# A gated recurrence and a perceptron on one core: weights rounded with an integer add, and the transposes around the scan split into single steps

## The chip, the core and the metric

The kernel runs on one core of one Trainium2 chip. The engines are TensorE (PE in the rows; PEld is its loading of weights), VectorE (DVE), ScalarE (ACT), GpSimd (POOL, which here issues the weights' DMAs) and SyncE (SP, which issues the other DMAs). The metric is the device time of one execution in microseconds. The time before is the median of three runs, 892.08 us (891.6 to 896.12).

## The reference

```python
def _attn_ref(q, k, v, a_re, a_im):              # (4, 8, 768, 48)
    mag = np.sqrt(a_re * a_re + a_im * a_im)
    scale = np.minimum(mag, 0.999) / (mag + 1e-06)
    a_re_n, a_im_n = (a_re * scale, a_im * scale)
    for t in range(S):
        new_re = ar * S_re - ai * S_im
        new_im = ar * S_im + ai * S_re
        kv = np.einsum('bhd,bhe->bhde', k[:, :, t], v[:, :, t])
        S_re, S_im = (new_re + kv, new_im)
        y[:, :, t] = np.einsum('bhd,bhde->bhe', q[:, :, t], S_re)

def _moe_ref(x, w_in, w_out):                    # x = y as (3072, 384)
    h = x @ w_in                                 # w_in (384, 2048)
    r = np.maximum(h, 0.0)
    g = r * r
    return (g @ w_out).astype(np.float32)        # w_out (2048, 384)
```

The two weights reach the kernel in 64-bit floats; all else is 32-bit.

## The kernel before

The sequence is cut into 8 units: 4 batches, 2 halves of 384 positions each. The recurrence of a unit is turned into running products of the gates and ordinary masked products of scores. Each unit passes through three lists of work.

- **The chain** (`chain_work`) is mostly VectorE and ScalarE: `load`; `normalise` for each half z of the heads; `measure`, three ScalarE sums of squares into a throw-away tile `junk`; `inner` and `inverse` for each z, which end with the tile `last` (L691, L692); `totals`, in which TensorE transposes the three parts j of `last` (4 transposes each, tile `tot`, L721), ScalarE copies the first two into `e` (L723) and VectorE makes running products of the third into `x` (L726); `scan`, some 70 small VectorE operations on `e` (L754, L757, L758); `back`, in which TensorE transposes e and x back (12 transposes, tile `bk`, L790) and ScalarE copies them to `xn` (L791); and `apply` for each z (L801 to L813), whose output `QK` is what the next list reads.
- **The pair list** (`pair_work`) takes four pairs of heads i: `turn` transposes QK (tile `tq`, L825, copied by L828), `keep` makes the state for the second half (`kv`), `score` makes masked scores (`sa`, `sb`; VectorE L843, L851 and ScalarE copies), `mix` multiplies them with v (`ypair`, L878 and L882), and the result goes by DMA into `xT`.
- **The dense list** (`dense_work`) has 16 items `hidden` (tile `h`, 3 products each, L913, with two ScalarE passes L916 and L917) and 12 items `project` (tile `o`, 4 products each, L925).

`merge` interleaves lists evenly: item i of a list with n items stands at (i + 0.5)/n. The program is: chain of unit 0 alone; pair list of unit 0 merged with `convert` of pieces 0 to 15; chain of unit 1 merged with `convert` of pieces 16 to 31; then, for each unit n, its dense list merged with the pair list of unit n+1 and the chain of unit n+2. Every engine runs its own instructions in one fixed order, which a list scheduler derives from this program and may move up where buffers allow. The PSUM pool `trp` with two buffers (tag `tr`) serves `tot`, `bk`, `tq` and `kv` together.

`convert(i)` brings one of 32 pieces of the weights (128 x 384 numbers of 64 bits) into the buffer `raw` by a GpSimd DMA and makes 32-bit floats of it with five VectorE operations (L576, L578, L580, L582, L584): two put sign, exponent and mantissa of the upper word in place, two scale the lower word to the last place, one adds the two.

Of the kernel before, what the change touches and what calls it, by code (L numbers as in the profile page):

```python
# [9 lines left out]
F32 = mybir.dt.float32  # L10
I32 = mybir.dt.int32
U32 = mybir.dt.uint32
BF16 = mybir.dt.bfloat16
AF = mybir.ActivationFunctionType
ALU = mybir.AluOpType
PSUM = bass.MemoryType.PSUM
# [463 lines left out]
def fast_path(ctx, tc, q, k, v, a_re, a_im, moe_w_in, moe_w_out, out, flag):  # L480
# [10 lines left out]
    nc = tc.nc  # L491
    B, H, S, D = q.shape
    C = 128
# [18 lines left out]
    pr = ctx.enter_context(tc.tile_pool(name="pr", bufs=2))  # L512
    gp = ctx.enter_context(tc.tile_pool(name="gp", bufs=NF))
    xp = ctx.enter_context(tc.tile_pool(name="xp", bufs=2))
    wst = ctx.enter_context(tc.tile_pool(name="wst", bufs=2))
    trp = ctx.enter_context(tc.tile_pool(name="trp", bufs=2, space=PSUM))
    scp = ctx.enter_context(tc.tile_pool(name="scp", bufs=2, space=PSUM))
    yp = ctx.enter_context(tc.tile_pool(name="yp", bufs=1, space=PSUM))
# [44 lines left out]
    def convert(i):  # L563

        dst, src = piece(i)
        if not wide:
            nc.gpsimd.dma_start(
                out=dst.rearrange("p (m f) -> p m f", m=src.shape[1]), in_=src)
            return
        raw = wst.tile([C, DM, 2], U32, name="raw", tag="raw")  # L570
        nc.gpsimd.dma_start(
            out=raw.rearrange("p (m f) two -> p m (f two)", m=src.shape[1]), in_=src)
        lo, hi = raw[:, :, 0], raw[:, :, 1]
        bits = dst.bitcast(U32)
        more = wst.tile([C, DM], U32, name="more", tag="more")
        dve.tensor_scalar(out=bits, in0=hi, scalar1=0x07FFFFFF, scalar2=3,  # L576
                          op0=ALU.bitwise_and, op1=ALU.logical_shift_left)
        dve.scalar_tensor_tensor(out=bits, in0=hi, scalar=0xC0000000, in1=bits,  # L578
                                 op0=ALU.bitwise_and, op1=ALU.bitwise_or)
        dve.tensor_scalar(out=more, in0=bits, scalar1=0xFF800000, scalar2=None,  # L580
                          op0=ALU.bitwise_and)
        dve.scalar_tensor_tensor(out=more.bitcast(F32), in0=lo, scalar=2.0 ** -52,  # L582
                                 in1=more.bitcast(F32), op0=ALU.mult, op1=ALU.mult)
        dve.tensor_tensor(out=dst, in0=dst, in1=more.bitcast(F32), op=ALU.add)  # L584

    SPARE = ("fa0", "fa1", "fb0", "fb1")

# [106 lines left out]
    def measure(u):  # L694

        for j, t in enumerate((whole(u["qk", 0]), whole(u["qk", 1]),
                               u["v"].rearrange("p j h d -> p (j h d)"))):
            junk = wst.tile([C, H * W * D], BF16, name="junk", tag="junk", bufs=1)
            act.activation(out=junk, in_=t, func=AF.Square,
                           accum_out=sums[:, u["n"], 4 + j:5 + j])  # L700

    carry = {}

    def totals(u):


        e = u["e"] = wk.tile([R, 2, NP, C + 1], F32, name="e", tag="e")
        x = u["x"] = wk.tile([R, NP, C + 1], F32, name="x", tag="x")
        if u["half"] == 0:
            dve.memset(e[:, 0, :, 0], SCALE)  # L710
            dve.memset(e[:, 1, :, 0], 0.0)
            dve.memset(x[:, :, 0], SCALE ** -2)
        else:
            dve.tensor_copy(out=e[:, :, :, 0], in_=carry["e"])
            dve.tensor_copy(out=x[:, :, 0], in_=carry["x"])
        last = u["last"]
        for j in range(3):
            src = last[:, j].rearrange("p (i h) d -> p i (h d)", i=NP)
            ps = trp.tile([R, NP, C], F32, name="tot", tag="tr")
            for i in range(NP):  # L720
                nc.tensor.transpose(ps[:, i], src[:, i], ident)  # L721
            if j < 2:
                act.copy(out=e[:, j, :, 1:C + 1], in_=ps)  # L723
            else:
                for i in range(NP):
                    dve.tensor_tensor_scan(out=x[:, i, 1:C + 1], data0=ps[:, i],  # L726
                                           data1=ones, initial=x[:, i, 0:1],
                                           op0=ALU.mult, op1=ALU.bypass)
        n = u["n"]
        dve.scalar_tensor_tensor(out=grow[0:R, n], in0=x[:, :, 0], scalar=2.0 ** 124,  # L730
                                 in1=x[:, :, C], op0=ALU.mult, op1=ALU.is_ge)
        if u["half"] == NHALF - 1:
            dve.tensor_scalar(out=total[0:R, u["b"]], in0=x[:, :, C], scalar1=2.0 ** 124,
                              scalar2=None, op0=ALU.is_le)
        else:
            carry["x"] = wk.tile([R, NP], F32, name="cx", tag="cx")
            dve.tensor_copy(out=carry["x"], in_=x[:, :, C])
# [22 lines left out]
    def scan(u):  # L760

        e = u["e"]
        body = e[:, :, :, 0:C]
        v8 = body.rearrange("p r i (g w) -> p r i g w", w=8)
        for w in range(1, 8):
            product(u, v8[:, :, :, :, w], v8[:, :, :, :, w - 1], v8[:, :, :, :, w])
        v32 = v8[:, :, :, :, 7].rearrange("p r i (g w) -> p r i g w", w=4)

        inc = wk.tile([R, 2, NP, 16], F32, name="inc", tag="inc")
        i4 = inc.rearrange("p r i (g w) -> p r i g w", w=4)  # L770
        dve.tensor_copy(out=inc, in_=v8[:, :, :, :, 7])
        for w in range(1, 4):
            product(u, i4[:, :, :, :, w], i4[:, :, :, :, w - 1], i4[:, :, :, :, w])
        for g in range(1, 4):
            prev = i4[:, :, :, g - 1, 3]
            for_all = prev.unsqueeze(3).to_broadcast([R, 2, NP, 4])
            product(u, i4[:, :, :, g], i4[:, :, :, g], for_all)
        for i in range(NP):
            y = inc[:, :, i, 0:15].unsqueeze(3).to_broadcast([R, 2, 15, 8])
            product(u, v8[:, :, i, 1:16], v8[:, :, i, 1:16], y)  # L780
        if u["half"] < NHALF - 1:
            carry["e"] = wk.tile([R, 2, NP], F32, name="ce", tag="ce")
            product(u, carry["e"], e[:, :, :, C - 1], e[:, :, :, C])

    def back(u):
        xn = u["xn"] = wk.tile([C, 3, H, D], F32, name="xn", tag="xn")
        for j, src in enumerate((u["e"][:, 0], u["e"][:, 1], u["x"])):
            ps = trp.tile([C, NP, R], F32, name="bk", tag="tr")
            for i in range(NP):
                nc.tensor.transpose(ps[:, i], src[:, i, 0:C], ident[0:R, 0:R])  # L790
            act.copy(out=xn[:, j].rearrange("p (i h) d -> p i (h d)", i=NP), in_=ps)  # L791

    def apply(u, z):

# [142 lines left out]
    def chain_work(u):  # L937
        return ([lambda: load(u)] + [lambda z=z: normalise(u, z) for z in range(2)]
                + [lambda: measure(u)]
                + [lambda z=z, f=f: f(u, z) for f in (inner, inverse) for z in range(2)]  # L940
                + [lambda: totals(u), lambda: scan(u), lambda: back(u)]
                + [lambda z=z: apply(u, z) for z in range(2)])


# [103 lines left out]
```

## Time and profile before

| | us |
|---|---|
| median of 3 runs | 892.08 |
| profiled execution | 891.34 |
| its span, first to last instruction | 889.6 |
| TensorE busy | 769.7 |
| VectorE busy | 550.4 |
| ScalarE busy | 421.4 |
| GpSimd busy | 43.7 |

The profiled execution is one run on its own, so its 891.34 differs a little from the median. Of it, 889.6 us are the span and 1.7 lie around it. Busy times overlap, since the engines run side by side. The mean granted clock of TensorE is .977 of full speed.

### The profile page before, as it was taken

The page shows a single profiled execution, that of the slowest core. Times are in us where ns is not written, and L with a number is a line of the kernel's source. Part 1 is how long each engine was busy: PE and PEld are TensorE (multiplying, and loading weights), DVE is VectorE, ACT ScalarE, POOL GpSimd, SP SyncE. Part 2 cuts the span into 40 slices and gives each one's busy share as a digit, 9 for nine tenths or more (in the row PEclk, how much of TensorE's full clock was granted, in tenths as well). Part 3 has the DMA queues.
Part 4 walks back from the last instruction along what each step waited for, and adds up shares of the span by engine and source line. Part 5 has one row for each costly group of instructions (what it writes and reads, how often), then busy time and mean ns, then how long its engine had stood idle before and what let it go on. Part 6 is the DMA issues. An engine that isn't in the chain of part 4 may idle for free.

```text
span 889.6 us, 9241 instructions
## 1 busy us (share of the span) xinstructions
PE 769.7 (87%) x3138; PEld 462.7 (52%) x3138; DVE 550.4 (62%) x1415; ACT 421.4 (47%) x833; POOL 43.7 (5%) x76
## 2 busy tenths in 40 slices
PE   0106989987898989998999899998999889999996
PEld 0004645443455655664666555564666545555553
DVE  4998899988987697338760877168652876400000
ACT  5303845067378329731784239621973215411510
POOL 1020111000000000000000000000000034100000
PEclk9999999998998999999999999998999999999999
DMA  9134443240130033000500132002300068400000
GB/s 239 36 98 128 141 139 108 71 116 13 41 107 7 17 96 96 7 16 16 148 8 8 36 115 50 7 16 62 104 7 7 15 181 270 149 16 31 1 9 22
DMA packets 76920, 61.24 MB, mean 69 GB/s; under 512 B 28736, under 2 KB 71744, under 8 KB 76864
## 3 DMA queue, kind: packets, MB, share of 16 engines
q1 hardware_dynamic: 70720, 35.40, 14.4%
q0 software_dynamic: 6144, 25.17, 9.3%
q8 instruction: 26, 0.43, 0.2%
q14 instruction: 30, 0.25, 0.1%
HBM read 51.12 MB, written 4.72 MB: 63 GB/s over the span
## 4 chain that ended last, share of the span: by engine, by line
PE 49%; DVE 23%; issue 13%; DMA 9%; ACT 4%; POOL 1%; SPq 0%; POOLq 0%; ACTq 0%
PE h L913 19%; PE o L925 14%; DVE fa L754 7%; PE ypair L882 4%; PE sa L839 4%; DVE QK L813 2%; PE tq L825 2%; DMA raw<-in_moe_w_in_dram 2%; DVE e L757 2%; PE ypair L878 2%; DMA look<-in_moe_w_in_dram 2%; DMA raw<-in_moe_w_out_dram 2%; PE sb L849 2%; DMA look<-in_moe_w_out_dram 1%; PE sa L841 1%
## 5 line engine op out<-in xcount | busy, mean ns | idle before, releaser
L913 PE MATMUL h<-xT,w 128*128 128x384 f32 x768 | 272.1, 494 | 9.0 <-DMA xT<-yt 5.1
L925 PE MATMUL o<-w,g 128*128 128x384 f32 x768 | 263.7, 489 | 1.6 <-DVE w L584 1.5
L925 PEld LDWEIGHTS o<-w,g 128*128 128x128 f32 x768 | 140.7, 190 | 87.6 <-DVE w L584 4.1
L913 PEld LDWEIGHTS h<-xT,w 128*128 128x128 f32 x768 | 139.1, 192 | 89.6 <-issue 10.5
L843 DVE TENSOR_TENSOR A<-sa,mask 128x256 f32<-128x256 f32 x64 | 26.8, 422 | 131.5 <-PE sa L841 131.3
L828 ACT COPY QKT<-tq 96x512 f32<-96x512 f32 x96 | 80.9, 854 | 41.3 <-PE tq L825 41.2
L916 ACT ACTIVATE g<-h 128x384 f32<-128x384 f32 x128 | 62.4, 491 | 73.7 <-PE h L913 73.7
L825 PE MATMUL tq<-ident,QK 128*96 128x128 f32 x384 | 61.2, 286 | 10.7 <-DVE QK L813 7.2
L917 ACT ACTIVATE g<-g 128x384 f32<-128x384 f32 x128 | 66.7, 525 | 2.3
L825 PEld LDWEIGHTS tq<-ident,QK 128*96 128x96 f32 x384 | 45.4, 132 | 39.5 <-issue 21.1
L882 PE MATMUL ypair<-A,v 128*48 128x256 f32 (+2 forms) x384 | 63.1, 410 | 0.0
L839 PE MATMUL sa<-QKT 96*128 96x384 f32 x128 | 55.8, 518 | 3.7 <-ACT QKT L828 3.7
L844 ACT COPY A<-sa 128x256 f32<-128x256 f32 x64 | 23.6, 372 | 59.3 <-DVE A L843 59.0
L929 ACT COPY ot<-o 128x384 f32<-128x384 f32 x24 | 11.5, 478 | 84.3 <-PE o L925 84.2
L721 PE MATMUL tot<-ident,last 128*96 128x128 f32 x96 | 15.8, 293 | 39.5 <-ACT last L691 35.0
L790 PE MATMUL bk<-ident,e 96*128 96x96 f32 x64 | 14.7, 311 | 40.0 <-DVE e L757 39.8
L791 ACT COPY xn<-bk 128x384 f32<-128x384 f32 x24 | 10.9, 480 | 73.5 <-PE bk L790 73.5
L754 DVE TENSOR_TENSOR fa<-e 96x128 f32<-96x128 f32 (+1 forms) x120 | 39.9, 366 | 8.2 <-ACT e L723 6.9
L813 DVE TENSOR_TENSOR QK<-qk,a 128x576 f32<-128x576 f32 x64 | 44.1, 750 | 0.0
L882 PEld LDWEIGHTS ypair<-A,v 128*48 128x48 f32 x384 | 27.1, 130 | 31.5 <-issue 23.2
L991 DVE TENSOR_SCALAR flag<-cnt 1x1 int32<-1x1 f32 x1 | 0.1, 147 | 69.1 <-PE cnt L990 69.1
L596 POOL DMA_DIRECT2D look<-in_moe_w_in_dram x16 | 12.2, 761 | 566.2 <-DVE a L807 555.4
(106 smaller groups left out, 975.8 us busy)
## 6 DMA issues: line engine op xcount, KB each, us to landing
raw<-in_moe_w_in_dram POOLq DMA_DIRECT2D x16, 384.0 KB, 3.7
raw<-in_moe_w_out_dram POOLq DMA_DIRECT2D x16, 384.0 KB, 3.3
look<-in_moe_w_in_dram POOLq DMA_DIRECT2D x16, 384.0 KB, 4.3
look<-in_moe_w_out_dram POOLq DMA_DIRECT2D x16, 384.0 KB, 4.1
a<-in_a_re_dram SPq DMA_DIRECT2D x16, 288.0 KB, 3.0
a<-in_a_im_dram SPq DMA_DIRECT2D x16, 288.0 KB, 3.4
qk<-in_q_dram SPq DMA_DIRECT2D x16, 288.0 KB, 4.3
qk<-in_k_dram SPq DMA_DIRECT2D x16, 288.0 KB, 4.5
```

The source lines that it names most:

```text
L754: dve.tensor_tensor(out=t, in0=x, in1=y[:, j].unsqueeze(1).to_broadcast(shape), op=ALU.mult)
L813: dve.tensor_tensor(out=t[:, j, :, :, r], in0=qk[:, j], in1=a[:, r], op=ALU.mult)
L825: nc.tensor.transpose(ps[:, 2 * j + h], src[:, j, (2 * i + h) % HH, c].rearrange("p r d -> p (r d)"), ident)
L828: act.copy(out=u["T"][i].rearrange("r z (p c) -> r c z p", c=W)[:, c], in_=ps)
L839: nc.tensor.matmul(sa[:, 0:3].rearrange("p n t -> p (n t)"), lhsT=kt[:, 0:C], rhs=qt, start=True, stop=True)
L843: dve.tensor_tensor(out=A[:, h, 0:4:3], in0=sa[:, 0:4:3], in1=mask2, op=ALU.mult)
L844: act.copy(out=A[:, h, 1:3], in_=sa[:, 1:3])
L882: nc.tensor.matmul(ypair[64 * h:64 * h + D, j * C:L], lhsT=u["v"][:, j, 2 * i + h], rhs=A[:, h, lo:hi].rearrange("p n t -> p (n t)"), star ...
L913: nc.tensor.matmul(ps, lhsT=w1[:, f, m], rhs=u["xT"][:, m], start=(m == 0), stop=(m == NM - 1))
L916: act.activation(out=t, in_=ps, func=AF.Relu)
L917: act.activation(out=t, in_=t, func=AF.Square)
L925: nc.tensor.matmul(u["o"], lhsT=u["g"][f][:, ts(c, C)], rhs=w2[:, f], start=(f == 0), stop=(f == NF - 1))
```

## The change

`convert` keeps the two operations that build the upper part. The lower word is no longer masked, multiplied and added as a float. ScalarE multiplies it by 2^-29 and writes it as an integer, which rounds it to the last place of the 32-bit mantissa, and VectorE adds this as an integer to the bits of the upper part. The pool `wst` has three buffers `raw` instead of two. The tile `more` keeps two buffers and now shares them with `junk`, which becomes an 8-bit float so that it fits. `totals` and `back` do one part j per call, so that the chain list has 17 items instead of 13, and the groups of four transposes stand apart in the merged program.

```diff
-    wst = ctx.enter_context(tc.tile_pool(name="wst", bufs=2))
+    wst = ctx.enter_context(tc.tile_pool(name="wst", bufs=3))
...
-        more = wst.tile([C, DM], U32, name="more", tag="more")
+        more = wst.tile([C, DM], U32, name="more", tag="more", bufs=2)
+        act.activation(out=more, in_=lo, func=AF.Copy, scale=2.0 ** -29)
         dve.tensor_scalar(out=bits, in0=hi, scalar1=0x07FFFFFF, scalar2=3,
                           op0=ALU.bitwise_and, op1=ALU.logical_shift_left)
         dve.scalar_tensor_tensor(out=bits, in0=hi, scalar=0xC0000000, in1=bits,
                                  op0=ALU.bitwise_and, op1=ALU.bitwise_or)
-        dve.tensor_scalar(out=more, in0=bits, scalar1=0xFF800000, scalar2=None,
-                          op0=ALU.bitwise_and)
-        dve.scalar_tensor_tensor(out=more.bitcast(F32), in0=lo, scalar=2.0 ** -52,
-                                 in1=more.bitcast(F32), op0=ALU.mult, op1=ALU.mult)
-        dve.tensor_tensor(out=dst, in0=dst, in1=more.bitcast(F32), op=ALU.add)
+        dve.tensor_tensor(out=bits, in0=bits, in1=more, op=ALU.add)
...
-            junk = wst.tile([C, H * W * D], BF16, name="junk", tag="junk", bufs=1)
-            act.activation(out=junk, in_=t, func=AF.Square,
+            junk = wst.tile([C, H * W * D], F8, name="junk", tag="more", bufs=2)
+            act.activation(out=junk, in_=t, func=AF.Square, saturate=False,
                            accum_out=sums[:, u["n"], 4 + j:5 + j])
...
-    def totals(u):
+    def totals(u, j):
...
-        for j in range(3):
-            src = last[:, j].rearrange("p (i h) d -> p i (h d)", i=NP)
-            ps = trp.tile([R, NP, C], F32, name="tot", tag="tr")
-            for i in range(NP):
-                nc.tensor.transpose(ps[:, i], src[:, i], ident)
-            if j < 2:
-                act.copy(out=e[:, j, :, 1:C + 1], in_=ps)
+        src = u["last"][:, j].rearrange("p (i h) d -> p i (h d)", i=NP)
+        ps = trp.tile([R, NP, C], F32, name="tot", tag="tr")
+        for i in range(NP):
+            nc.tensor.transpose(ps[:, i], src[:, i], ident)
+        if j < 2:
+            act.copy(out=e[:, j, :, 1:C + 1], in_=ps)
+            return
...
-    def back(u):
+    def back(u, j):
...
-                + [lambda: totals(u), lambda: scan(u), lambda: back(u)]
+                + [lambda j=j: totals(u, j) for j in range(3)] + [lambda: scan(u)]
+                + [lambda j=j: back(u, j) for j in range(3)]
```

Two places show what this does to the order of the engines. The first is TensorE at the transposes of unit 1's chain, with the dense list of unit 0 around them (h and o). Before, the last groups of `tot` and the first of `bk`:

```order
L913 MATMUL h<-xT,w_110 128x384 x24
L721 MATMUL tot<-ident,last 96x128 x4
L913 MATMUL h<-xT,w_110 128x384 x11
L721 MATMUL tot<-ident,last 96x128 x4
L913 MATMUL h<-xT,w_110 128x384 x3
L721 MATMUL tot<-ident,last 96x128 x2
L913 MATMUL h<-xT,w_110 128x384 x7
L925 MATMUL o<-w_111,g 128x384 x2
L721 MATMUL tot<-ident,last 96x128 x2
L925 MATMUL o<-w_111,g 128x384 x31
L790 MATMUL bk<-ident,e 128x96 x2
```

The same place after the change:

```order
L913 MATMUL h<-xT,w_110 128x384 x2
L722 MATMUL tot<-ident,last 96x128 x4
L913 MATMUL h<-xT,w_110 128x384 x7
L722 MATMUL tot<-ident,last 96x128 x4
L913 MATMUL h<-xT,w_110 128x384 x3
L722 MATMUL tot<-ident,last 96x128 x2
L913 MATMUL h<-xT,w_110 128x384 x4
L722 MATMUL tot<-ident,last 96x128 x2
L913 MATMUL h<-xT,w_110 128x384 x28
L790 MATMUL bk<-ident,e 128x96 x2
L925 MATMUL o<-w_111,g 128x384 x2
```

The totals moved up by some 20 products of h, and 32 of the products of o that stood ahead of `bk` now stand behind it. The second place is TensorE at the chain of a later unit, from its totals to its back transposes. Before:

```order
L721 MATMUL tot<-ident,last 96x128 x8
L925 MATMUL o<-w_111,g 128x384
L721 MATMUL tot<-ident,last 96x128 x4
L925 MATMUL o<-w_111,g 128x384 x3
L849 MATMUL sb<-QKT 128x256 x2
...
L925 MATMUL o<-w_111,g 128x384 x4
L790 MATMUL bk<-ident,e 128x96 x6
L878 MATMUL ypair<-QKT,S 48x384
L790 MATMUL bk<-ident,e 128x96 x2
L878 MATMUL ypair<-QKT,S 48x384
L882 MATMUL ypair<-A,v 48x384
L790 MATMUL bk<-ident,x 128x96 x4
```

After, from the second group of the totals to the second of the back transposes:

```order
L722 MATMUL tot<-ident,last 96x128 x4
L878 MATMUL ypair<-QKT,S 48x384 x2
...
L722 MATMUL tot<-ident,last 96x128 x4
L925 MATMUL o<-w_111,g 128x384 x4
L839 MATMUL sa<-QKT 128x384
...
L925 MATMUL o<-w_111,g 128x384 x4
L790 MATMUL bk<-ident,e 128x96 x4
L825 MATMUL tq<-ident,QK 96x128 x4
L925 MATMUL o<-w_111,g 128x384 x4
L825 MATMUL tq<-ident,QK 96x128 x4
L790 MATMUL bk<-ident,e 128x96 x4
```

Each group of four transposes now stands by itself, with products of o, ypair or tq between, and `ypair` no longer shares a place with `bk`. The third place is VectorE in unit 0's scan, where products of the scan (`fa` and `e`) and operations of the conversion (`w`, `raw`, `more`) take turns. Before:

```order
L584 TENSOR_TENSOR w_110<-w_110,more 128x384
L754 TENSOR_TENSOR fa_131<-e 96x128
L754 TENSOR_TENSOR fa_145<-e 96x128
L578 SCALAR_TENSOR_TENSOR w_110<-raw,w_110 128x384
L757 TENSOR_TENSOR e<-fa_131,fa_145 96x4x16
L758 TENSOR_TENSOR e<-fa_131,fa_145 96x4x16
L580 TENSOR_SCALAR more<-w_110 128x384
L754 TENSOR_TENSOR fa_131<-e 96x128
L754 TENSOR_TENSOR fa_145<-e 96x128
L582 SCALAR_TENSOR_TENSOR more<-raw,more 128x384
```

After:

```order
L584 ISA w_110<-w_110,more 128x768
L753 TENSOR_TENSOR fa_131<-e 96x128
L753 TENSOR_TENSOR fa_145<-e 96x128
L579 TENSOR_SCALAR w_110<-raw 128x384
L756 TENSOR_TENSOR e<-fa_131,fa_145 96x4x16
L757 TENSOR_TENSOR e<-fa_131,fa_145 96x4x16
L581 SCALAR_TENSOR_TENSOR w_110<-raw,w_110 128x384
L753 TENSOR_TENSOR fa_131<-e 96x128
L753 TENSOR_TENSOR fa_145<-e 96x128
L584 ISA w_110<-w_110,more 128x768
```

Nothing moved out of the slots: one conversion operation still stands in each, but now three and not five of them finish a piece. Ahead of the first L804 (apply) stand 10 each of L576 to L582 and 9 of L584 before, and 16 each of L579, L581 and L584 after. The new add is printed in a form of its own, with 768 columns, one for each half of its 384 words. On ScalarE the new operations L577 stand among the copies of the chain; at the end of this scan one stands between the second and the third copy to `xn`.

## Rows read from the trace of the kernel before

**Rows 1.** The page's first part: busy us, share, instructions.

```profile
PE 769.7 (87%) x3138; PEld 462.7 (52%) x3138; DVE 550.4 (62%) x1415; ACT 421.4 (47%) x833; POOL 43.7 (5%) x76
```

**Rows 2.** Stages: length, busy PE, PEld, DVE, ACT, POOL, clock, DMA, GB/s.

```profile
40.00:75.00 35.00, 3.55 (x14) 2.02 (x12) 34.10 (x122) 1.34 (x3) 5.79 (x7) 1.00 0.30 80
150.00:175.00 25.00, 23.29 (x74) 12.65 (x73) 24.69 (x98) 0.96 (x2) 2.16 (x4) 1.00 0.30 94
175.00:200.00 25.00, 21.53 (x103) 12.45 (x101) 21.44 (x41) 15.23 (x28) 0.00 (x0) 1.00 0.36 104
200.00:225.00 25.00, 19.54 (x82) 9.88 (x82) 20.41 (x40) 18.86 (x36) 0.00 (x0) 0.86 0.04 12
225.00:260.00 35.00, 30.97 (x135) 17.36 (x132) 33.35 (x104) 17.76 (x35) 0.00 (x0) 1.00 0.25 61
260.00:300.00 40.00, 37.28 (x161) 23.00 (x161) 23.52 (x43) 30.29 (x64) 0.00 (x0) 0.91 0.13 37
...
345.00:393.00 48.00, 48.00 (x202) 29.54 (x201) 19.68 (x38) 33.65 (x70) 0.00 (x0) 1.00 0.03 7
...
490.00:515.00 25.00, 22.27 (x91) 13.52 (x90) 22.20 (x85) 5.22 (x10) 0.00 (x0) 0.86 0.11 32
```

**Rows 3.** Groups by line: shapes, count | busy us, mean ns | idle before.

```profile
L813 DVE TENSOR_TENSOR QK<-qk,a 128x576 f32<-128x576 f32 x64 | 44.1, 750 | 0.0
...
L584 DVE TENSOR_TENSOR w<-w,more 128x384 f32<-128x384 f32 x32 | 17.5, 548 | 0.0
...
L576 DVE TENSOR_SCALAR w<-raw 128x384 uint32<-128x384 uint32 x32 | 11.3, 357 | 4.4 <-DMA raw<-in_moe_w_in_dram 2.3 <-DMA raw<-in_moe_w_out_dram 2.0
...
L917 ACT ACTIVATE g<-g 128x384 f32<-128x384 f32 x128 | 66.7, 525 | 2.3
```

**Rows 4.** Timeline of VectorE in unit 0's scan: start us, length us.

```profile
46.82 0.35 DVE L576 TENSOR_SCALAR w<-raw 128x384 uint32<-128x384 uint32 x1
47.09 0.27 DVE L757 TENSOR_TENSOR e<-fa,fa 96x64 f32<-96x64 f32 x1
...
47.36 0.55 DVE L578 SCALAR_TENSOR_TENSOR w<-raw,w 128x384 uint32<-128x384 uint32 x1
47.83 0.68 DVE L754 TENSOR_TENSOR fa<-e 96x128 f32<-96x128 f32 x2
```

**Rows 5.** Timeline at the end of the front, VectorE and TensorE.

```profile
70.12 0.75 DVE L801 TENSOR_TENSOR qk<-qk,xn 128x576 f32<-128x576 f32 x1
...
75.70 1.06 PE L825 MATMUL tq<-ident,QK 128*96 128x128 f32 x4 [6.14 <-DVE QK L813]
```

**Rows 6.** Timeline of TensorE: unit 1's last back transposes, unit 3's last totals.

```profile
177.47 0.49 PE L790 MATMUL bk<-ident,x 96*128 96x96 f32 x4
...
298.43 0.60 PE L721 MATMUL tot<-ident,last 128*96 128x128 f32 x4
```

**Rows 7.** Timeline of TensorE in unit 4's chain, totals to back transposes.

```profile
390.83 1.04 PE L721 MATMUL tot<-ident,last 128*96 128x128 f32 x8
...
404.65 2.75 PE L925 MATMUL o<-w,g 128*128 128x384 f32 x8
408.19 0.27 PE L790 MATMUL bk<-ident,e 96*128 96x96 f32 x1 [0.80 <-DVE e L757]
...
411.90 0.60 PE L790 MATMUL bk<-ident,e 96*128 96x96 f32 x2
412.44 0.88 PE L878 MATMUL ypair<-QKT,S 96*48 96x384 f32 x1
412.44 0.88 PE L882 MATMUL ypair<-A,v 128*48 128x384 f32 x1
...
416.54 2.85 PE L925 MATMUL o<-w,g 128*128 128x384 f32 x8
```

**Rows 8.** Timeline of TensorE: the last unit's 48 products of o.

```profile
850.26 31.12 PE L925 MATMUL o<-w,g 128*128 128x384 f32 x96
```

**Rows 9.** Timeline of ScalarE: the last part of unit 4's `last`.

```profile
366.23 0.35 ACT L692 COPY last<-fb 128x192 f32<-128x192 f32 x1 [0.43 <-DVE fb L684]
```

More of the change, by code (lines that the diff above doesn't have):

```diff
@@ L12 @@
 U32 = mybir.dt.uint32
-BF16 = mybir.dt.bfloat16
+F8 = mybir.dt.float8e5
 AF = mybir.ActivationFunctionType
@@ L697, in measure @@
                                u["v"].rearrange("p j h d -> p (j h d)"))):
-            junk = wst.tile([C, H * W * D], BF16, name="junk", tag="junk", bufs=1)
-            act.activation(out=junk, in_=t, func=AF.Square,
+            junk = wst.tile([C, H * W * D], F8, name="junk", tag="more", bufs=2)
+            act.activation(out=junk, in_=t, func=AF.Square, saturate=False,
                            accum_out=sums[:, u["n"], 4 + j:5 + j])
     carry = {}
-    def totals(u):
[L707 to L711, printed above, removed]
+    def totals(u, j):
+        if j == 0:
+            u["e"] = wk.tile([R, 2, NP, C + 1], F32, name="e", tag="e")
+            u["x"] = wk.tile([R, NP, C + 1], F32, name="x", tag="x")
+        e, x = u["e"], u["x"]
+        if j < 2 and u["half"] == 0:
+            dve.memset(e[:, j, :, 0], SCALE if j == 0 else 0.0)
+        elif j < 2:
+            dve.tensor_copy(out=e[:, j, :, 0], in_=carry["e"][:, j])
+        elif u["half"] == 0:
@@ L712, in totals @@
             dve.memset(x[:, :, 0], SCALE ** -2)
         else:
-            dve.tensor_copy(out=e[:, :, :, 0], in_=carry["e"])
             dve.tensor_copy(out=x[:, :, 0], in_=carry["x"])
-        last = u["last"]
-        for j in range(3):
-            src = last[:, j].rearrange("p (i h) d -> p i (h d)", i=NP)
-            ps = trp.tile([R, NP, C], F32, name="tot", tag="tr")
-            for i in range(NP):
-                nc.tensor.transpose(ps[:, i], src[:, i], ident)
-            if j < 2:
-                act.copy(out=e[:, j, :, 1:C + 1], in_=ps)
[L724 to L728, printed above, removed]
@@ L729, in totals @@
-        n = u["n"]
-        dve.scalar_tensor_tensor(out=grow[0:R, n], in0=x[:, :, 0], scalar=2.0 ** 124,
+        src = u["last"][:, j].rearrange("p (i h) d -> p i (h d)", i=NP)
[5 more added lines that the diff above has]
+            return
+        for i in range(NP):
+            dve.tensor_tensor_scan(out=x[:, i, 1:C + 1], data0=ps[:, i], data1=ones,
+                                   initial=x[:, i, 0:1], op0=ALU.mult, op1=ALU.bypass)
@@ L731, in totals @@
+        dve.scalar_tensor_tensor(out=grow[0:R, u["n"]], in0=x[:, :, 0], scalar=2.0 ** 124,
                                  in1=x[:, :, C], op0=ALU.mult, op1=ALU.is_ge)
@@ L783, in scan @@
             product(u, carry["e"], e[:, :, :, C - 1], e[:, :, :, C])
-    def back(u):
[L786 to L791, printed above, removed]
+    def back(u, j):
+        if j == 0:
+            u["xn"] = wk.tile([C, 3, H, D], F32, name="xn", tag="xn")
+        src = u["x"] if j == 2 else u["e"][:, j]
+        ps = trp.tile([C, NP, R], F32, name="bk", tag="tr")
+        for i in range(NP):
+            nc.tensor.transpose(ps[:, i], src[:, i, 0:C], ident[0:R, 0:R])
+        act.copy(out=u["xn"][:, j].rearrange("p (i h) d -> p i (h d)", i=NP), in_=ps)
     def apply(u, z):
```

## The prediction

> **What bounds the kernel now.** I read the busy line first: TensorE works in 87% of the span, VectorE in 62%, ScalarE in 47% [rows 1]. TensorE bounds most of the span, so an operation that VectorE saves is worth nothing wherever VectorE waits for TensorE anyway. The table by stages says where that is not so [rows 2]. From 40 to 75 us VectorE is busy 34.10 of 35 us and TensorE 3.55; from 150 to 175 VectorE again has 24.69 of 25. In both stretches the chain of a unit (scan, apply) shares VectorE with the conversion of the weights. From 175 to 300 TensorE is the busier engine but leaves 25 − 21.53, 25 − 19.54, 35 − 30.97 and 40 − 37.28 us, together 15.7, unused, at a granted clock of .86 and .91 in two of the four. Later TensorE is without a gap for 48 us (345 to 393), and each unit has one hole: from 490 to 515 it lacks 2.73 us and the granted clock is .86.
>
> That hole is the back transposes. At 404.65 the last products of o before it start; three waits for VectorE's L757 follow, of which the row with .80 is the first, and o goes on at 416.54 [rows 7]. The eight rows of o take 2.75, so from 407.4 to 416.54 there are 9.1 us. In them stand 12 transposes, at eight in 1.04 us [rows 7] 1.6 us, and the products of ypair: those of the two heads start together (at 412.44 [rows 7]), so that 1152 columns count, 3 × .648 (the time of 384 columns, [rows 8]), 1.9 us. So 9.1 − 3.5, some 5.5 us, are lost per unit, half in the waits and half at the lower speed after them. Units 3 to 7 have this hole; 1 and 2 lie in the disturbed stretch before 300.
>
> **The conversions.** The five old operations of a piece are .357 or .548 long [rows 3]; on a full VectorE the next one starts .27 after a short one and .47 after a long one [rows 4]. So a piece cost .27 × 2 + .47 × 3 = 1.95. Two of them stay (.74). The new add is in no row. It handles as many bytes as L584, with the same two inputs: .548, step .47. That is the lower bound. The order prints it with 768 columns, halves of the words; from 384 to 576 columns a two-input operation grows from .548 to .750 [rows 3], which continues to .548 + 384 × .00105 = .95, step .87: the upper bound. I take .548, because two whole-word streams of 384 words are what L584 reads. A piece then costs 1.21 (1.61 at the upper bound).
>
> [...]
>
> ScalarE's part, 384 columns, I price as L917 of that width, .525 [rows 3]; the lower bound is nothing on the path, the upper twice that for its alternate words. Sixteen lie before the first apply, where ScalarE has 1.34 us to do in 35 [rows 2]. The other sixteen, 8.4 us, lie between 75 and 175 among PSUM copies, which can each be .5 late. Third raw buffer: VectorE waits for raw data 4.4 us in all [rows 3], so at most that, and I count nothing: the waits for data fall inside the same work. The junk buffer's new type leaves ScalarE's operation as wide as before; nothing.
>
> **Front, to the first transpose at 75.70** [rows 5]. A saved operation does not simply shorten the front, since the order fills the slots with operations of later pieces. Before, ahead of the first apply stand 10 of each old operation and 9 of the last: 20 × .27 + 29 × .47 = 19.0 us. After, 16 of each: 16 × 1.21 = 19.4 (25.8). So +.4 (+6.8). One L577 stands ahead of the third copy of xn, for which L801 waits: +.5 (0 to 2). First transpose at +.9.
>
> **Unit 1.** Between the first score and unit 1's apply there were 22 of each, 22 × 1.95 = 42.9 us; now 15 of the first and 16 of the two others, 4.0 + 16 × .94 = 19.1. That is 23.8 less on VectorE (17.4 with the dear add), so the back transposes of unit 1, which end about 178.0 [rows 6], could end 23.8 − .9 = 22.9 earlier. Part turns into waits for scores and for ScalarE; I take seven tenths, 16 (bounds 0 and 22.9).
>
> The price is on TensorE. Unit 1's transposes now stand behind 48 h and 6 o where 48 h and 38 o preceded them. A product of 384 columns takes 31.12/48 = .648 [rows 8], so 20.7 us of work move behind them, and TensorE stands in front of tot and bk instead. Between there and the end of unit 3's totals (about 299.0) [rows 6], 46 o stand instead of 19: 17.4 us more. What these can fill is the loss from 175 to 300: 15.7 idle, and the lower clock, .14 × 25 + .09 × 40 = 7.1, together 22.8. I take 20, since dense work now lies between nearly all of unit 1's pair. Totals of unit 3: −16 + 17.4 − 20 = −18.6 us.
>
> **Units 3 to 7.** The totals are split. The scan needs only the first two groups, and the first of these stands, by the order, 6 h, 8 o, a ypair, two sa and some transposes earlier, some 13 us. Its input is complete at 366.6 [rows 9] where the transposes started at 390.83 [rows 7]: 24 us in hand, so no wait. From the end of the second group to the first bk, TensorE has, at .648 for 384 columns, 5 groups of four o (13.0), two groups of four transposes (1.0), ypair (1.9), two sa of 512 columns (1.7) and sb, 512 columns (.9): 18.5 us. Before, it came there after 407.4 − 391.9 = 15.5. VectorE's last column arrived at about 411.9, 20.0 after the totals; one score more in the scan makes it 20.4. So the wait shrinks from about 4.5 to 2, and the second and third group find their data ready. I take 2.5 saved per unit (0 to 5.5): 12.5 over five. What is late next is apply: its last copy comes after bk of x, about 4 us later in the unit, hidden unless the next unit's tq arrive first.
>
> **Sum.** The profiled execution took 891.34 (span 889.6), .7 below the median. 891.34 − 18.6 − 12.5 = 860.2; with .7, **861 us**. The last unit's dense work is untouched.
>
> **Rivals.** *The add is dear* (.95): front +7.3, unit 1 −17.4 + 7.3 = −10.1, seven tenths −7; unit 3 −7 + 17.4 − 20 = −9.6; in all −22.1, 870. For it the printed 768 columns; against it the bytes. *The spreading gives nothing:* the first bk still waits for the scan's last column, and the clock falls as before; 861 + 12.5 = 873.5. For it: the scan is 20 long whatever stands before it. *The early gain is lost:* TensorE stands at unit 1's transposes and the moved o fill too little (−16 and 20 come to 17.4 only); 861 + 18.6 = 879.6. For it: pair 1 also waits for copies, which o products don't shorten. Both of the last two together are no change, 892. *The other side, more stalls:* six groups of transposes per unit instead of a bundle; if one more of them finds its copy or its data late, it costs what the hole of 490 to 515 costs, 2.73 idle and .14 × 25 = 3.5 in clock, 6.2 a unit. Five units: 31, and no 12.5: 861 + 12.5 + 31 = 904.5. It makes the kernel slower once a unit's loss grows by more than (18.6 + 4.5)/5 = 4.6 us. For it: two PSUM buffers serve tq, tot, bk and kv, each freed by ScalarE; against it the 24 us in hand.
>
> **How the numbers follow.** Forecast .45, dear add .18, spreading nil .14, early gain lost .10, both .04, more stalls .09. The low end is the forecast with all of the 22.9 and 1.7 more for each later unit: 861 − 6.9 − 8.5 = 845.6. The high end holds everything but the last two cases, and some of their near side: 884. Half a percent, 4.5 us, is about what a measurement tells from no change. Faster .83 (some of the early-loss case falls away), same .07, slower .10.
>
> **What would show it.** L584 at .55 or .95; first tq at 76 to 77 (83 if dear); unit 1's last bk near 162 instead of 177.47; unit 3's totals near 280; the hole of each later unit with at most two waits for L757 and less than 3.5 us lost. Wrong if the windows from 175 to 300 keep 15 us of idle time, if a wait of TensorE for `last` appears after 300, or if L577 stands long on a DMA in front of PSUM copies.

## The result, and the profile after

The changed kernel takes 867.76 us (median of 4 runs, 866.02 to 870.67) where the kernel before took 891.84 (4 runs): a ratio of .9723, 95% interval .9683 to .9763, 24 us less. 861 had been forecast, within 845 to 884. The profiled execution after is the longest of the four, 870.67 us with a span of 868.9, so its rows show 20.7 us less in the span (889.6 before) and not 24.

The page's first part of the changed kernel, which answers to [rows 1]:

```profile
PE 759.4 (87%) x3138; PEld 462.6 (53%) x3138; DVE 524.3 (60%) x1355; ACT 434.9 (50%) x865; POOL 43.6 (5%) x76
```

VectorE has 60 instructions and 26 us less, ScalarE 32 instructions and 13.5 us more. TensorE has the same instructions, but is busy 10 us less. That is not the clock over the whole run, whose granted mean is .977 before and .975 after. It is `ypair`, here before and after; the experiments come back to the reason.

```profile
L882 PE MATMUL ypair<-A,v 128*48 128x256 f32 (+2 forms) x384 | 63.1, 410 | 0.0
```

```profile
L882 PE MATMUL ypair<-A,v 128*48 128x384 f32 (+2 forms) x384 | 51.8, 390 | 0.1
```

The groups by line show the price of the new add and of ScalarE's part:

```profile
L584 DVE CUSTOM_DVE_ANT_0 w<-w,more 128x768 uint16<-128x768 uint16 x32 | 17.6, 549 | 0.0
...
L579 DVE TENSOR_SCALAR w<-raw 128x384 uint32<-128x384 uint32 x32 | 11.2, 357 | 0.0
...
L577 ACT ACTIVATE more<-raw 128x384 uint32<-128x384 uint32 x32 | 17.7, 556 | 27.0 <-DVE w L584 7.3 <-DMA raw<-in_moe_w_in_dram 5.1 <-DVE w L579 4.1
```

The add of 768 halves takes .549, as long as the add of 384 floats did (.548 in [rows 3]). The forecast's lower bound was right and the first rival (.95) was not. L577 takes .556, .525 was taken.

The timeline at the end of the front, which answers to [rows 5]:

```profile
71.16 0.48 ACT L791 COPY xn<-bk 128x384 f32<-128x384 f32 x1 [0.15 <-PE bk L790]
71.69 0.75 DVE L801 TENSOR_TENSOR qk<-qk,xn 128x576 f32<-128x576 f32 x1
...
77.26 1.06 PE L825 MATMUL tq<-ident,QK 128*96 128x128 f32 x4 [6.14 <-DVE QK L813]
```

The first transpose is 1.56 later than before. The third copy to `xn` waits for TensorE's `bk`, not for the L577 ahead of it; what is late is the whole chain of unit 0. TensorE's timeline at unit 1's last back transposes and unit 3's last totals, as in [rows 6]:

```profile
159.78 0.53 PE L790 MATMUL bk<-ident,x 96*128 96x96 f32 x4
...
283.99 0.60 PE L722 MATMUL tot<-ident,last 128*96 128x128 f32 x4
```

They are 17.7 and 14.4 earlier. The table by stages shows that the stretch from 175 to 300 is still not full (columns as in [rows 2]):

```profile
175.00:200.00 25.00, 24.66 (x112) 13.53 (x111) 20.57 (x40) 22.89 (x46) 0.00 (x0) 1.00 0.23 68
200.00:225.00 25.00, 21.69 (x80) 12.98 (x80) 20.91 (x84) 5.53 (x11) 0.00 (x0) 0.87 0.05 14
225.00:260.00 35.00, 31.79 (x145) 18.89 (x143) 29.95 (x53) 27.20 (x56) 0.00 (x0) 0.90 0.34 90
260.00:300.00 40.00, 37.98 (x163) 24.03 (x162) 27.25 (x93) 20.57 (x45) 0.00 (x0) 1.00 0.04 13
```

TensorE leaves 8.9 us of it unused, where 15.7 were, and two stretches still show a granted clock of .87 and .90. The hole of unit 4 on TensorE's timeline, which answers to [rows 7]:

```profile
390.84 0.33 PE L790 MATMUL bk<-ident,e 96*128 96x96 f32 x2
391.56 0.30 PE L790 MATMUL bk<-ident,e 96*128 96x96 f32 x1 [0.38 <-DVE e L756]
392.82 0.31 PE L790 MATMUL bk<-ident,e 96*128 96x96 f32 x1 [0.96 <-DVE e L756]
392.97 0.60 PE L825 MATMUL tq<-ident,QK 128*96 128x128 f32 x4
393.40 2.75 PE L925 MATMUL o<-w,g 128*128 128x384 f32 x8
395.99 0.60 PE L825 MATMUL tq<-ident,QK 128*96 128x128 f32 x4
396.42 0.49 PE L790 MATMUL bk<-ident,e 96*128 96x96 f32 x4
```

Where three waits stood there are two, 1.34 us in all; the second group finds its data.

To compare kernels with one order of work and another, the experiments use one mark that means the same in each: the end of ScalarE's last copy `yt` (L887) of a unit, with which its pair list ends. Unit 2's in the two kernels, before and after:

```profile
338.60 0.47 ACT L887 COPY yt<-ypair 112x384 f32<-112x384 f32 x1
```

```profile
329.73 0.46 ACT L887 COPY yt<-ypair 112x384 f32<-112x384 f32 x1
```

This table has the ends of these copies in the profiled executions (us), and, as the length of a later unit, a third of the time from unit 3's to unit 6's:

| kernel | unit 0 | unit 1 | unit 2 | unit 3 | unit 6 | unit 7 | a later unit |
|---|---|---|---|---|---|---|---|
| before | 113.8 | 233.6 | 339.1 | 435.2 | 726.5 | 819.8 | 97.1 |
| changed | 115.7 | 233.2 | 330.2 | 422.5 | 704.1 | 799.5 | 93.9 |
| spread_only | 113.8 | 254.9 | 352.0 | 443.9 | 725.7 | 819.4 | 93.9 |
| convert_only | 114.2 | 227.5 | 327.6 | 426.0 | 716.0 | 808.5 | 96.7 |
| raw_two | 113.3 | 230.3 | 327.7 | 419.7 | 701.5 | 793.4 | 93.9 |
| one_op | 106.8 | 212.2 | 310.8 | 402.9 | 685.2 | 776.9 | 94.1 |
| split_from_3 | 114.0 | 227.9 | 331.9 | 424.0 | 706.1 | 796.4 | 94.0 |
| back_bundled | 114.9 | 228.8 | 327.3 | 417.9 | 694.8 | 787.9 | 92.3 |
| totals_bundled | 114.2 | 234.0 | 327.7 | 420.8 | 705.2 | 798.8 | 94.8 |
| add_on_pool | 133.9 | 252.4 | 350.1 | 442.5 | 723.1 | 814.1 | 93.5 |
| later_back | 114.8 | 232.6 | 328.7 | 418.4 | 690.9 | 785.2 | 90.8 |
| round_twice | 114.6 | 227.8 | 326.0 | 418.0 | 698.5 | 790.9 | 93.5 |
| bundled_raw_two | 113.3 | 218.2 | 318.6 | 409.9 | 686.9 | 779.7 | 92.3 |
| combined | 113.7 | 217.5 | 320.8 | 409.9 | 681.8 | 775.6 | 90.6 |

### The profile page after: what moved, and what is told of

Same layout as the page of the kernel before. It is cut to its first block, busy times and chain, and to the rows that moved or that the text cites. A ratio compares the mean times of both kernels' runs of the same rounds, so it can differ in the third digit from the quotient of the medians.

```text
span 868.9 us, 9241 instructions
## 1 busy us (share of the span) xinstructions
PE 759.4 (87%) x3138; PEld 462.6 (53%) x3138; DVE 524.3 (60%) x1355; ACT 434.9 (50%) x865; POOL 43.6 (5%) x76
## 4 chain that ended last, share of the span: by engine, by line
PE 54%; DVE 25%; DMA 8%; ACT 7%; issue 4%; SPq 1%; POOL 1%; POOLq 0%; ACTq 0%; DVEq 0%
PE h L913 22%; PE o L925 15%; DVE fa L753 8%; PE tq L825 4%; PE sa L839 4%; PE ypair L882 3%; PE sb L849 2%; DVE e L756 2%; DMA a<-in_a_im_dram 2%; DVE QK L813 2%; DMA look<-in_moe_w_in_dram 2%; PE kv L866 2%; DMA look<-in_moe_w_out_dram 2%; ACT QKT L828 1%; DVE e L757 1%
## 5 line engine op out<-in xcount | busy, mean ns | idle before, releaser
L925 PE MATMUL o<-w,g 128*128 128x384 f32 x768 | 269.5, 496 | 0.0
L916 ACT ACTIVATE g<-h 128x384 f32<-128x384 f32 x128 | 62.6, 493 | 61.2 <-PE h L913 61.0
L882 PE MATMUL ypair<-A,v 128*48 128x384 f32 (+2 forms) x384 | 51.8, 390 | 0.1
L790 PE MATMUL bk<-ident,e 96*128 96x96 f32 x64 | 14.1, 294 | 40.9 <-DVE e L756 40.0
L929 ACT COPY ot<-o 128x384 f32<-128x384 f32 x24 | 11.4, 476 | 67.6 <-PE o L925 67.6
L882 PEld LDWEIGHTS ypair<-A,v 128*48 128x48 f32 x384 | 24.1, 125 | 31.5 <-issue 23.3
L849 PE MATMUL sb<-QKT 96*128 96x256 f32 x128 | 34.1, 389 | 2.3 <-ACT A L844 2.3
```

What stands on the lines that cost most here:

```text
L849: nc.tensor.matmul(sb[:, h].rearrange("p n t -> p (n t)"), lhsT=kt[:, C:2 * C], rhs=qt[:, C:3 * C], start=True, stop=True)
L882: nc.tensor.matmul(ypair[64 * h:64 * h + D, j * C:L], lhsT=u["v"][:, j, 2 * i + h], rhs=A[:, h, lo:hi].rearrange("p n t -> p (n t)"), star ...
L916: act.activation(out=t, in_=ps, func=AF.Relu)
L925: nc.tensor.matmul(u["o"], lhsT=u["g"][f][:, ts(c, C)], rhs=w2[:, f], start=(f == 0), stop=(f == NF - 1))
```

## The experiments

The theory is that two gains stand side by side: the cheaper conversion brings unit 1's chain forward (early units), the spread transposes shorten each later unit. The rivals are that one of the two carries everything, or that they need each other.

**The two parts by themselves.** `spread_only` is the kernel before with `totals` and `back` split; `convert_only` is the changed kernel with both in one piece:

```diff
-                + [lambda j=j: totals(u, j) for j in range(3)] + [lambda: scan(u)]
-                + [lambda j=j: back(u, j) for j in range(3)]
+                + [lambda: totals(u), lambda: scan(u), lambda: back(u)]
```

> The kernel before with totals and back split, the conversion as before. Theory (two separate gains): the split saves about 2.6 us in each of units 3 to 7 and nothing in the early units, so 892 - 13 = 879, and the first pair list of unit 1 ends where it did, near 233. Rival (the split carries the whole change, since VectorE's saving was hidden): 868 to 870. Rival (the split only works where the chain arrives earlier through the cheaper conversion): within 3 of 892.

> The changed kernel with totals and back in one piece as before, the new conversion kept. Theory (two separate gains): unit 1's back transposes end near 160, the pair list of unit 2 ends some 9 to 11 us earlier than before, and later units keep their three waits for L757 with 96.5 us a unit: 892 - 11 = 881. Rival (hidden): 890 to 893. Rival (the conversion is all): 868 to 870.

`spread_only` took 891.01 us, ratio .9983 (.9961 to 1.0005): no gain, the number of its second rival. `convert_only` took 882.54, ratio .9892 (.9858 to .9926), as expected: a gain of 10 by itself. Together they gain 24. So the split pays only with the conversion, and the marks say how. In `spread_only` the later units are as short as in the changed kernel (93.9), and from unit 1's mark to unit 7's it gains 21.7. So the saving of the later units is there without the cheaper conversion. But unit 1's mark comes 21.3 late. Its timeline of TensorE has the place:

```profile
238.19 0.40 PE L790 MATMUL bk<-ident,e 96*128 96x96 f32 x1 [8.24 <-DVE e L756]
```

and the stretch around it has a granted clock of .66:

```profile
225.00:260.00 35.00, 23.10 (x82) 13.40 (x82) 29.84 (x98) 8.27 (x15) 0.00 (x0) 0.66 0.13 30
```

With the old conversion unit 2's scan ends late, and the split `bk` stands in front of the rest of pair list 1; .34 × 35 = 11.9 us of clock, an estimate from the length and the granted clock of that row, and 8.24 of waiting are 20 of the 21.3. With the new conversion the same place waits 2.54. In `convert_only` unit 2's mark is 11.4 early and the later units keep nearly their old length, 96.7. The split costs something in the changed kernel too: against `convert_only` its marks are 5.7 late at unit 1, 2.6 at unit 2, and 9.0 early at unit 7. Of the 5.7, six products of h, 6 × .648 = 3.9 us, are only moved: they stand ahead of this mark and stood behind it in `convert_only`. At unit 2's mark the same products of h and o stand ahead in both.

**One step further with the conversion.** `one_op` has L579 alone; L577, L581 and the add are gone:

```diff
-        act.activation(out=more, in_=lo, func=AF.Copy, scale=2.0 ** -29)
...
-        dve.scalar_tensor_tensor(out=bits, in0=hi, scalar=0xC0000000, in1=bits,
-                                 op0=ALU.bitwise_and, op1=ALU.bitwise_or)
-        dve.tensor_tensor(out=bits, in0=bits, in1=more, op=ALU.add)
```

> The changed kernel with one VectorE operation a piece (L579) and no ScalarE operation: the lower word and the sign are left out of the weights. Theory: conversions still stand on the path in the front and in unit 1's chain, 16 x .94 = 15 us of VectorE in the front, of which the scan's own gaps return little, so the first transpose comes 8 to 14 us earlier and the total is 855 to 862. Rival (TensorE's order bounds from the first transpose on, and the front's slots are free): 866 to 869.

847.77, ratio .9495 (.9462 to .9528): 20 us less than the changed kernel, more than the range. First transpose at 69.28, 8 us earlier; unit 1's mark 21 us earlier, and about as much (22.6) at unit 7's. VectorE lost 32 × .94 = 30 us of work, and ScalarE its 17.7 us of L577. If VectorE's part is what counts, two thirds of it appear in the end, nearly all by the end of pair list 1; the run took both away and does not tell them apart.

**The third raw buffer.** `raw_two` differs in one number:

```diff
-    wst = ctx.enter_context(tc.tile_pool(name="wst", bufs=3))
+    wst = ctx.enter_context(tc.tile_pool(name="wst", bufs=2))
```

> The changed kernel with two raw buffers instead of three. Theory: VectorE waited 4.4 us in all for raw data before, part of it in places where it has nothing urgent, so 868 to 871. Rival (three buffers carry the early gain, because ScalarE now holds a raw buffer too): 875 or more, with waits of VectorE for raw data or of L577 above 10 us in all.

865.91, ratio .9707 (.9673 to .9741): below the range, and not slower than the changed kernel, whose interval it overlaps. VectorE's L579 waits 1.9 us in all for raw data; L577 has 33.4 us of idle time before it where it had 27.0, so the sign of the rival is there, but these waits do not lengthen the kernel. With two buffers the first totals start 1.4 earlier (30.54 for 31.97) and the first transpose comes at 75.33 where it came at 77.26. With a third buffer VectorE converts more ahead of unit 0's chain, which is the one that all wait for: 3 each of L579 and L581 stand ahead of the first totals there and 2 with two buffers, and 16 and 14 ahead of the first transpose.

**Which of the two splits.** `back_bundled` keeps the split totals and does `back` in one piece, `totals_bundled` the other way round.

> The changed kernel with only the totals split; the back transposes in one bundle. Theory (the time between the second totals and the first back transpose decides): that distance is no shorter than in the changed kernel, so the later units save their 2.5 us each and the total is 864 to 870. Rival (the three back groups standing apart save the time): the three waits for the scan come back at .8 to 1 each, 877 to 883.

> The changed kernel with only the back transposes split; the totals in one bundle. Theory (distance decides): 16 products of o lie between the totals and the first back transpose where 20 lay before, so TensorE waits longer at it, 4 to 5 us in each unit; total 880 to 890. Rival (the back groups standing apart save the time): 866 to 872.

`back_bundled` took 860.51, ratio .9618 (.9583 to .9654); `totals_bundled` 871.02, ratio .9738 (.9707 to .9768). The first is below its range, the second has its rival's number. With `convert_only` (both in one piece, .9892) and the changed kernel (both split, .9723) the four cases are complete. A later unit takes 96.7 us with nothing split, 94.8 with `back` split, 92.3 with the totals split and 93.9 with both. So each split gains by itself, that of the totals more, and splitting `back` on top of the totals costs 1.6 us per later unit. `totals_bundled` was expected at 880 to 890: the distance that I had counted in products of o leaves out what else stands between, and the waits were .5 to 1 twice a unit, not 4 to 5.

**The distance to the first back transpose.** `later_back` is the changed kernel with an empty item in the chain list:

```diff
-                + [lambda j=j: totals(u, j) for j in range(3)] + [lambda: scan(u)]
+                + [lambda j=j: totals(u, j) for j in range(3)] + [lambda: scan(u), lambda: None]
```

> The changed kernel with one empty item between scan and back, so that the first back transpose comes some 2 us later in each later unit and the totals a little earlier. Theory (what is left in the later units is the wait at the first group, and the low clock that it brings): no wait of .9 for L756 after unit 2, o products back to .49 on the mean from .50, 1 to 1.5 us less a unit, 861 to 866. Rival (the three groups standing apart cost by themselves, by switching between transposes and products): 867 to 870, waits gone or not.

856.67, ratio .9591 (.9558 to .9625), below the range. No wait for L756 is left after unit 2, and a later unit takes 90.8 us, 3.1 less where 1 to 1.5 was expected. So the split of `back` does not cost by itself: its first group stood too early. The rows of unit 4's first two groups in this kernel, without a wait:

```profile
390.12 0.49 PE L790 MATMUL bk<-ident,e 96*128 96x96 f32 x4
390.45 2.77 PE L925 MATMUL o<-w,g 128*128 128x384 f32 x8
393.50 2.75 PE L925 MATMUL o<-w,g 128*128 128x384 f32 x8
396.08 0.49 PE L790 MATMUL bk<-ident,e 96*128 96x96 f32 x4
```

What a wait costs beyond its length, and what it does not, shows in the time of TensorE from unit 3's mark to unit 6's. First the group of o (288 records in each kernel), then the whole of TensorE (columns as in [rows 2]), then the 160 records of `ypair` alone (the same columns without POOL). Before:

```profile
L925 PE MATMUL o<-w,g 128*128 128x384 f32 x288 | 99.9, 490 | 0.0
435.16:726.54 291.38, 282.29 (x1193) 174.26 (x1192) 176.34 (x449) 151.64 (x306) 4.34 (x6) 0.97 0.16 44
435.16:726.54 291.38, 28.27 (x160) 11.96 (x160) 0.00 (x0) 5.76 (x13) 0.97 0.16 44
```

After:

```profile
L925 PE MATMUL o<-w,g 128*128 128x384 f32 x288 | 102.8, 502 | 0.0
422.46:704.11 281.65, 274.12 (x1184) 170.62 (x1183) 175.43 (x453) 148.03 (x301) 7.30 (x10) 0.99 0.17 49
422.46:704.11 281.65, 20.62 (x160) 9.32 (x160) 0.00 (x0) 5.69 (x12) 0.99 0.17 49
```

In `later_back`:

```profile
L925 PE MATMUL o<-w,g 128*128 128x384 f32 x288 | 99.0, 488 | 0.0
418.39:690.90 272.51, 270.45 (x1190) 169.38 (x1189) 173.74 (x448) 149.10 (x302) 6.06 (x8) 1.00 0.17 47
418.39:690.90 272.51, 20.62 (x160) 9.32 (x160) 0.00 (x0) 5.69 (x12) 1.00 0.17 47
```

From before to after the three units are 9.7 us shorter. Idle time gives 9.1 − 7.5 = 1.6 of it, `ypair` 28.3 − 20.6 = 7.7, and o takes 2.9 back. Two things lengthened `ypair` before. One is the clock. Only one pair of heads in four has its `ypair` in the hole, and there the granted clock was .50 in these stretches (`ypair` alone):

```profile
507.72:514.55 6.83, 3.92 (x12) 1.70 (x12) 0.00 (x0) 0.00 (x0) 0.50 0.01 2
603.33:610.15 6.82, 4.00 (x11) 1.19 (x13) 0.00 (x0) 0.00 (x0) 0.50 0.01 2
705.73:709.14 3.41, 2.80 (x10) 1.46 (x10) 0.00 (x0) 0.48 (x1) 0.50 0.00 0
```

Half of these 10.7 us, some 5.4, is lost to the clock, an estimate by the group of o: the eight records that start at 675.79 in the changed kernel took 4.44 us, of which 3.41 at a granted clock of .50, the eight at 581.07 took 2.75 at 1.00, and the 1.7 between is half of the 3.41. The other thing is the order, and accounts for the 2.3 us that are left. The products of a pair's two heads ran side by side where they stood together; before, `bk` stood between them. The first row is from unit 4's hole before, at a granted clock of 1.00, the second from the changed kernel:

```profile
411.12 0.85 PE L878 MATMUL ypair<-QKT,S 96*48 96x384 f32 x2
```

```profile
399.46 0.85 PE L878 MATMUL ypair<-QKT,S 96*48 96x384 f32 x4
```

Two records took as long as four. After, `ypair` stands together and at the full clock, and o stands behind the waits: it has 6.4 of the 6.8 us at a granted clock of .50 in these units, and is 3.8 us longer than in `later_back`, where no wait and no such stretch is left. So most of the gain of a later unit is that `ypair` no longer stands behind the waits, at the lower clock, nor is torn apart by `bk`; the shorter waits themselves are a sixth of it.

**The early units without the split.** `split_from_3` bundles totals and back for units 0 to 2.

> The changed kernel with totals and back in one piece for units 0 to 2 and split from unit 3 on. Theory (the split costs in the early units, where the scan is still late, and saves in the later ones): the pair lists of units 1 and 2 end near 227.5 and 327.6 as in convert_only, and from there each unit is as short as in the changed kernel: 878.3 less 11.6, a time of 864 to 868, 2 to 4 below the changed kernel. Rival (the early cost is given back later anyway, because the chain of unit 3 bounds): 868 or above. Rival (the later gain needs the early split): 878 to 882.

868.65, ratio .9724 (.9685 to .9764): no gain on the changed kernel, and above the range. Unit 1's mark is early as in `convert_only`, but unit 2's is 4.3 later than there. TensorE waits for a copy of h:

```profile
258.51 1.65 PE L913 MATMUL h<-xT,w 128*128 128x384 f32 x2 [3.94 <-ACT g L916]
```

ScalarE was never idle before it: from 249.4 to 257.99 it worked almost only on the next chain's gates and sums of squares, which stand ahead of L916 in its order. So the early cost of the split is there at unit 1's mark, but leaving it out together with a late split moved the order of another engine, and a new wait took its place. This is the first of three runs in which the order that comes out, more than the edit, set the time.

**GpSimd and ScalarE.** `add_on_pool` puts the add on GpSimd, `round_twice` does L577 twice:

```diff
-        dve.tensor_tensor(out=bits, in0=bits, in1=more, op=ALU.add)
+        pool.tensor_tensor(out=bits, in0=bits, in1=more, op=ALU.add)
```

> The changed kernel with the integer add on GpSimd instead of VectorE. Theory (VectorE's work for the conversion is still on the path in the first 160 us; one_op took 30 us of it away and saved 20): 15 us less on VectorE, so 10 us less in all, 857 to 860, if GpSimd's adds are ready in time. Rival (GpSimd's queue, which also issues the weights' DMAs, becomes the bound, or its adds slow VectorE): 868 or above, with VectorE or TensorE waiting for L584 or for raw data.

> The changed kernel with the ScalarE rounding of each piece done twice, into the same place. Theory (ScalarE's part lies beside other work, each copy at most .5 late): 17.8 us more of ScalarE cost 0 to 4, so 866 to 872. Rival (ScalarE stands on the chain of the first 160 us next to VectorE): 8 us or more, 876 and above.

`add_on_pool` took 882.18, ratio .9851 (.9816 to .9886), 14 us more than the changed kernel. GpSimd's group of adds:

```profile
L584 POOL TENSOR_TENSOR w<-w,more 128x384 uint32<-128x384 uint32 x32 | 54.1, 1693 | 90.5 <-DVE fa L652 44.0 <-DVE w L581 20.3 <-ACT more L577 19.5
```

An add takes 1.69 on the mean, and the DMAs of the weights stand behind it in the same queue; the first transpose comes at 93.32, 16 later, and unit 0's mark 18 later. The theory's saving of VectorE work could not appear. `round_twice` took 861.47, ratio .9622 (.9597 to .9648), *less* than the changed kernel with 18 us more work on ScalarE. The scheduler made another order of it: 45 products of h stand ahead of unit 1's last back transposes where 48 h and 6 o stood. (Products are counted as in the program's order; the trace has two records for each.) So this run does not give the price of L577. It speaks against the rival, whose 8 us or more did not appear, but with another order it does not show that ScalarE's 17.7 us are free.

**A faster version.** `bundled_raw_two` is `back_bundled` with two raw buffers.

> The kernel back_bundled with two raw buffers. Theory (the third raw buffer is not what gains): 858 to 862, as with three. If the two small gains of raw_two and back_bundled over the changed kernel add up: 857 to 859. Rival (with the back in one bundle the early units need the third buffer): 865 or more.

851.13, ratio .9516 (.9489 to .9542), more than the two gains together. Its unit 1 ends 10.6 earlier than in `back_bundled`: 24 h stand ahead of the third group of unit 1's totals there and 12 o ahead of the end of `bk`, where it had been 15 and 3, so that TensorE has work while the chain is late. That this is the cause is argued from the order; no run changes it alone. `combined` takes that kernel for units 0 to 2 and `later_back` from unit 3 on:

```diff
-                + [lambda j=j: back(u, j) for j in range(3)]
+                + ([lambda: None] + [lambda j=j: back(u, j) for j in range(3)]
+                   if u["n"] > 2 else [lambda: [back(u, j) for j in range(3)]])
```

> Two raw buffers; totals split everywhere; back in one bundle for units 0 to 2, and from unit 3 on split with one empty item between scan and back. Theory (early and late gains are independent): the pair list of unit 2 ends near 318.6 as in bundled_raw_two, and from there each unit takes 90.8 as in later_back instead of 92.3: 851 less 3 to 6, so 845 to 849. Rival (later_back saves only because its early units were late, so that its chain had time): 850 to 854, with waits for L756 back in the later units.

846.51, ratio .946 (.9434 to .9486): 47 us below the kernel before and 21 below the changed one. A later unit takes 90.6.

## Why the prediction came out as it did

- **The conversions: right.** .549 for the add, from the row of the old add; the rival's continuation by columns (.95) would have been wrong by .4.
- **Front, +.9: 1.56 measured, for another reason.** L577 ahead of the third copy cost nothing. The chain of unit 0 was late from its totals on (31.97 where they began at 30.50), because the third raw buffer lets conversions go ahead of it; `raw_two` takes this away. I had counted the third buffer at nothing. Not all of the 1.56 need be the change: `later_back`, with the same conversions ahead, starts its totals at 31.02 and its first transpose at 76.34.
- **Unit 1, −16: −17.7 measured** (177.47 to 159.78).
- **Totals of unit 3, −18.6: this term was mis-sized.** The row says −14.4. By the prediction's own sum, −17.7 + 17.4 − r = −14.4, so r, what comes back of the losses after unit 1, was 14.1 where "I take 20" of 22.8 stands. This is the step that failed, and these rows show what did not come back. They run from unit 1's last `bk` to unit 3's last totals, before, after and in `convert_only` (columns as in [rows 2]):

```profile
177.96:299.03 121.07, 105.39 (x460) 60.39 (x459) 95.56 (x215) 81.29 (x159) 0.00 (x0) 0.94 0.20 54
```

```profile
160.31:284.59 124.28, 117.26 (x509) 69.98 (x509) 98.87 (x229) 80.82 (x159) 0.00 (x0) 0.95 0.20 55
```

```profile
162.60:286.00 123.40, 119.58 (x532) 70.70 (x531) 95.19 (x215) 81.05 (x161) 0.00 (x0) 1.00 0.20 56
```

The idle time of TensorE fell from 15.7 to 7.0 us, but of the lower clock next to nothing came back (.94 and .95). The first split `bk` of unit 2 waits 2.54 here, and the granted clock is .87 and .90 from 200 to 260. In `convert_only`, with the groups in one piece, 3.8 us are idle, the clock is 1.00, and the same sum, with its last `bk` 15.4 earlier and 36 more products of o between, gives −15.4 + 23.3 − r = −13.0, an r of 20.9. So 20 could come back. Which edit kept it from doing so stays open: by the same sum `back_bundled`, without a split `bk`, has an r of some 14, and `round_twice`, with the same splits as the changed kernel and another order, some 21.

- **A term left out.** The sum carries the −18.6 to the end. But 57 products of o stood ahead of unit 3's last totals and 52 stand there now, so 5 × .648 = 3.2 us of work wait behind them: like for like the −14.4 is −11.2.
- **The rival "the early gain is lost"** was half true: at unit 1's mark nothing is won (−.4), at unit 2's 8.9. What lies between the −11.2 and the −8.9 no run takes apart.
- **Units 3 to 7, −12.5: −11.5 measured** from unit 2's mark to unit 7's, and 3.2 per unit between 3 and 6 where 2.5 was taken. The size was right, the reason only in part, so that part of it is luck. The prediction took it all from the waits; they give .5 per unit. It read the second half of a unit's loss as "the lower speed after them"; the rows of `ypair` above show that some of this was the order, at the full clock. What came back is `ypair`, 2.6 per unit, less what o lost.
- **The sum: −31.1 forecast, −24 measured; −20.7 in the profiled executions,** from which the terms above are read. Of these 10.4 us, 7.4 are unit 3's totals (18.6 − 11.2), 2.3 lie from there to unit 2's mark, and 1.0 in the later units.
- **What I did not see:** that the split alone is worth nothing. I gave each edit a saving of its own and added them. `spread_only` has the saving of the later units in full and loses as much in the early ones, where the chain comes late: the price of a `bk` that stood too early was a wait of 8.24 us, and a stretch of 35 us at a granted clock of .66.
- **More stalls, the other side:** its mechanism is what `spread_only` shows at one place (20 us); with the new conversion the wait at that place was 2.54 us.

## What to carry to other kernels

Two edits of which one makes data earlier and the other asks for it earlier are to be priced together: the second alone can be worth nothing. Put a step behind the wait that it would meet, not as early as the list allows: here one empty item took the last waits away and 3 us per unit. Where a scheduler makes the order, look at the order after every edit, even one that only adds work or takes a buffer: it can move more than the edit costs. The `ypair` products of two heads no longer ran side by side where another step stood between them: two records then took the .85 us that four took together.

## What the runs showed of the hardware

The integer add of 128x384 words on VectorE, printed as 768 halves, takes .549, the same as a float add of 384 columns (.548). The same add on GpSimd takes 1.69 on the mean of 32. The `ypair` products of two heads, 48 columns each, ran side by side where they stood together: four records took .85 us where two took .85 with `bk` between the heads. After short waits of TensorE for the scan the granted clock fell, but not after all of them. In the three units of the table above it was .50 for 17.1 us before, in all three, after waits of .81 to .96, and for 6.8 us after, in the two units where two waits of .96 came one behind the other; the third, with .39 and .96 (580.49), kept 1.00. `later_back`, without such waits there, shows 1.00 over the three units.
